# Parameter gradients of an S4 layer in a forward and backward kernel: two of their four groups computed during the second weights' gradient, from other buffers, with their scalings on VectorE

## The chip, the core and the metric

The kernel runs on one core of one Trainium2 chip. The metric is the device time of one execution in microseconds (us); of several executions the median counts, and less is better. A core has engines that work side by side, each in the order of its own instruction list: TensorE (PE in the profile, PEld for its weight loads), VectorE (DVE), ScalarE (ACT), GpSimd (POOL) and SyncE (SP). Here GpSimd and SyncE mostly issue DMAs, the transfers between the chip's memory (HBM) and the on-chip buffers (SBUF, 128 partitions). TensorE writes its results to banks of PSUM, from where VectorE or ScalarE must fetch them before a bank can be used again; such a fetch is called an evacuation.

## The reference, cut to what matters

A gated mixture of a state-space layer `a` and a two-layer network `b`, and the gradients of all its parameters:

```
g  = sigmoid((u * gate_w).sum(-1))                      # u: [1, 2048, 448] bf16
dt = exp(log_dt)[:, None];  A = A_re + i A_im; B, C likewise   # [448, 256]
K  = einsum("dn,dnl,dn->dl", C, exp(dt * A * l), dt * B).real
a  = irfft(rfft(u, 4096) * rfft(K, 4096))[:2048] + u * Dskip
b  = relu(u @ w1 + b1)**2 @ w2 + b2                     # 448 -> 1792 -> 448
y  = g * a + (1 - g) * b
outputs: y (out_0), and for a given grad_out the gradients of
u (out_1), A_re A_im B_re B_im C_re C_im (out_2..7), log_dt (out_8), Dskip (out_9),
w1 (out_10), b1 (out_11), w2 (out_12), b2 (out_13), gate_w (out_14)
```

What the change moves are out_2 to out_8. They are found for each of the 448 channels and 256 states from two complex sums over time, S and T, which the kernel has left in HBM earlier (s_d holds S and one part of T, t_d the other part), and from A, B, C and dt:

```
dB = dt*B;  W = C*dB                      (complex, 256 states wide)
dC = conj-product of dB and S;  dB-gradient = dt * conj-product of C and S
dA = dt * (W*T);   dlog_dt = sum over states of Re(W*S) + dt * Re(A*(W*T))
```

It is work for one elementwise engine: some 41 operations on tiles of 128 channels x 256 states, in four groups of 128, 128, 128 and 64 channels.

## The kernel before, in words

**How instructions get their order.** The kernel is written in a tile framework. A scheduler takes the program and lays down each engine's list: it follows the program's order as priority, but with its own estimate of times it may let a later instruction go first where an earlier one would wait. `tc.issue_after(x)` holds an instruction back in that schedule until x has been issued. Once laid down the order is fixed, and an engine stands still when the first instruction of its list has to wait. A buffer goes by a tag (`K.t("U16", ...)`): a new tile of the same tag may be written only when the last user of the old one is done.

**The stages.** Until some 660 us the kernel builds the convolution's kernel K and its spectrum, the network `b` and its hidden rows rT, the gradients' rows dhT, and the sums S and T. What the change touches comes after:

- The FFT of the kernel, fwd1 (L220) and fwd2 (L250), leaves the spectrum in the tile s1k. The end of fwd2 is interleaved with the products.
- `product(w, q)` (L1227): a complex multiplication of the spectra, `cmul` (L262 to L275, six VectorE operations of 128 x 1792 each), and `inv1` (L301), the first half of an inverse FFT on TensorE, whose result goes to HBM (hd, written from ScalarE's DMA queue). w is 0 for one of the two convolutions and 1 for the other, and q counts quarters. Products (0, 0..3) and (1, 0..1) stand in a row; products (1, 2) and (1, 3) stand in the loop of out_0.
- `grad_w2(j)` (L1180), j = 0 to 13, the second weights' gradient (out_12): `gradrows` (L1154) loads a block of rT by a 512 KB DMA from GpSimd's queue (L1166), TensorE turns it by 16 transposes (L1171), ScalarE squares it out of PSUM (L1172), TensorE does 16 matmuls (L1177) against the tile DB2, ScalarE copies the sum out (L1182), and GpSimd's queue stores it (L1183). VectorE has no part in it. DB2 lies in the buffer "U16".
- `grad_w1(j)` (L1186), j = 0 and 1: the same for the first weights, without the square. The other twelve blocks come at the very end.
- The parameter gradients' operands: A, B and C by twelve DMAs on GpSimd's queue (L1337, L1338: 192 KB for three groups together, 32 KB for the fourth) into the tile pgt, which takes over the buffer "U16" and so has to wait for the last matmul of grad_w2. `load_st` (L1235) brings s_d (512 KB a group) and t_d (256 KB) by SyncE's queue.
- `param_grads(dt)` (L1241): an add that completes T (L1250), two scalings of B by dt on ScalarE (L1261, L1262), the multiplications and additions on VectorE, two more scalings on ScalarE that write dA (L1271, L1272), the sum for dlog_dt, and six stores of 64 KB on GpSimd's queue (L1277). Groups 0 and 1 stand in the program after grad_w1(1) and ahead of the loop of out_0, groups 2 and 3 after that loop.
- The loop of out_0 (from L1356), four quarters: `inv2` (L325 to L332), the second half of the inverse FFT, of which the matmul L330 adds the network's part; and for each of four blocks of 128 rows two VectorE operations that read the bank (L1372, the row's dot product with grad_out, and L1373, the output). The text calls these "casts". A bank is free when both are done; two pairs of banks are in use.
- GU (L1389), one long multiplication on VectorE; then the loop of out_1, which is inv2 again with evacuations shared by ScalarE and VectorE (L1410); the turn of dlog (L1414), out_9 and out_14, and the other twelve blocks of grad_w1 (L1425 to L1433), half of each turned by a DMA transpose.

The scheduler weaves these together. In the trace the casts of out_0's first quarter run at 758.88, those of the second from 810.2, and the blocks of grad_w2 lie between them, one every 4.8 us. The scalings of group 0 stand in ScalarE's list among the evacuations of grad_w1, and the operations of group 0 in VectorE's list among the casts of out_0's third and fourth quarter.

Of the kernel before, what the change touches and what calls it, by code (L numbers as in the profile page):

```python
# [12 lines left out]
ACT = mybir.ActivationFunctionType  # L13
ALU = mybir.AluOpType
# [5 lines left out]
P = 128  # L20
L, D, N, F = 2048, 448, 256, 1792
LT = L // P
FT = F // P
DT = 4
# [313 lines left out]
def kernel(ctx, tc, A_u, A_A_re, A_A_im, A_B_re, A_B_im, A_C_re, A_C_im, A_log_dt, A_Dskip,  # L338
# [793 lines left out]
    K.pairs3 = False  # L1132
    K.fwd1(lambda j: xv[:, j], gd[2], stage= [b_[:, 1792 * i:1792 * i + 1792].rearrange("p (a d) -> p a d", d=D) for b_, n_ in ((Yv, 4), (Pk_, 4)) for i in range(n_)])
    lastw = row_block(3, ["X", "S", "F"])
    DB2 = K.t("U16", [P, LT, D])
    G_.dma_start(flat(DB2), bass.AP(tensor=DB_d, offset=0, ap=[[LT * D, P], [1, LT * D]]))
    U = K.t("D16", [P, LT, DP])
    G_.memset(U[:, :, D:D + 1], 1.0)
# [15 lines left out]
    def gradrows(w, j, nb):  # L1154

        nonlocal hi, ni
        late = w == 1 and j >= JL
        if late:
            raw_, hh = rl[hi % 2], hl[hi % 3]
            with tc.issue_after(lasths.ins):  # L1160
                nc.sync.dma_start_transpose(out=hh[:, 8:16], in_=bass.AP(tensor=dhT_d, offset=j * P * L + 1024, ap=[[L, P], [1, 1024]]))
        else:
            raw_, hh = hr[:, hi % 2], hn[:, hi % 2]
        hi += 1
        nl = L // 2 if late else L
        G_.dma_start(raw_, bass.AP(tensor=(rT_d if w == 0 else dhT_d), offset=j * P * L, ap=[[L, P], [1, nl]]))  # L1166
        for th in range(1 if late else 2):
            ps = K.ps(nb[ni % len(nb)], [P, 8, P], bf16)
            ni += 1
            for tt in range(8):  # L1170
                T_.transpose(ps[:, tt, :], raw_[:, (8 * th + tt) * P:(8 * th + tt + 1) * P], ident[:])  # L1171
            S.activation(hh[:, 8 * th:8 * th + 8, :], ps[:], ACT.Square if w == 0 else ACT.Copy)  # L1172
        ps = K.ps(nb[ni % len(nb)], [P, 512])
        ni += 1
        width = D if w == 0 else D + 1
        for t in range(LT):
            lastm = T_.matmul(ps[:, 0:width], lhsT=hh[:, t, :], rhs=(DB2[:, t, :] if w == 0 else U[:, t, 0:D + 1]), start=(t == 0), stop=(t == LT - 1))  # L1177
        return ps, lastm

    def grad_w2(j):  # L1180
        ps, lastm = gradrows(0, j, NB)
        S.copy(dw2s[:, j % 2], ps[:, 0:D])  # L1182
        G_.dma_start(out_12[j * P:(j + 1) * P, :], dw2s[:, j % 2])  # L1183
        return lastm
# [26 lines left out]
    def load_sx(w, q):  # L1211
        nonlocal nr
        t_ = ring[nr % 3]
        nr += 1
        nc.sync.dma_start(t_, bass.AP(tensor=sp_d[w], offset=q * 8 * D, ap=[[16 * 2 * D, P], [1, 8 * D]]))
        return t_.rearrange("p (a r d) -> p a r d", a=4, r=2)
# [10 lines left out]
    def product(w, q, sx):  # L1227
        K.cmul(Pk[:, q % 2], sx, spk(q), w == 1, Fc[:, 0:8 * D])
        K.inv1(Pk[:, q % 2], q, hd[1 + w])
# [11 lines left out]
    def param_grads(dt):  # L1241
        z = DSZ[dt]
        rows = slice(dt * P, dt * P + z)
        ob = Fc[:, 3584 + 1536 * (dt % 2):5120 + 1536 * (dt % 2)].rearrange("p (k n) -> p k n", k=6)
        ST, T1 = STs[dt], T1s[dt][:z]
        Ar, Ai, Br, Bi, Cr, Ci = (praw[:z, dt, i] for i in range(6))
        dBr, dBi, Wr, Wi, x1, x2, acc = (tmp[:z, i] for i in range(7))
        WTr, WTi = dBr, dBi
        V.tensor_tensor(out=ST[:z, 1], in0=ST[:z, 1], in1=T1, op=ALU.add)
        Sr, Si, Tr, Ti = ST[:z, 0, 0], ST[:z, 0, 1], ST[:z, 1, 0], ST[:z, 1, 1]  # L1250
        sc, nsc = dtc[:z, dt:dt + 1], ndtc[:z, dt:dt + 1]

        def mul(o_, a_, b_):
            V.tensor_tensor(out=o_, in0=a_, in1=b_, op=ALU.mult)  # L1254

        def sub(o_, a_, b_):
            V.tensor_tensor(out=o_, in0=a_, in1=b_, op=ALU.subtract)

        def stt(o_, a_, s_, b_, op1, **kw):
            V.scalar_tensor_tensor(out=o_, in0=a_, scalar=s_, in1=b_, op0=ALU.mult, op1=op1, **kw)  # L1260
        S.activation(dBr, Br, ACT.Copy, scale=sc)  # L1261
        S.activation(dBi, Bi, ACT.Copy, scale=sc)  # L1262
        mul(x1, Cr, dBr); mul(x2, Ci, dBi); sub(Wr, x1, x2)
        mul(x1, Cr, dBi); mul(x2, Ci, dBr); V.tensor_tensor(out=Wi, in0=x1, in1=x2, op=ALU.add)
        mul(x1, dBr, Sr); mul(x2, dBi, Si); sub(ob[:z, 4], x1, x2)
        mul(x1, dBr, Si); mul(x2, dBi, Sr); stt(ob[:z, 5], x1, -1.0, x2, ALU.subtract)
        stt(x1, Cr, sc, Sr, ALU.mult); stt(x2, Ci, sc, Si, ALU.mult); sub(ob[:z, 2], x1, x2)
        stt(x1, Cr, nsc, Si, ALU.mult); stt(x2, Ci, sc, Sr, ALU.mult); sub(ob[:z, 3], x1, x2)
        mul(x1, Wr, Tr); mul(x2, Wi, Ti); sub(WTr, x1, x2)
        mul(x1, Wr, Ti); mul(x2, Wi, Tr); V.tensor_tensor(out=WTi, in0=x1, in1=x2, op=ALU.add)  # L1270
        S.activation(ob[:z, 0], WTr, ACT.Copy, scale=sc)  # L1271
        S.activation(ob[:z, 1], WTi, ACT.Copy, scale=nsc)  # L1272
        mul(x1, Wr, Sr); mul(x2, Wi, Si); sub(acc, x1, x2)
        mul(x1, Ar, WTr); mul(x2, Ai, WTi); sub(x1, x1, x2)
        stt(x2, x1, sc, acc, ALU.add, accum_out=dlog[:z, dt:dt + 1])
        for i, o_ in enumerate((out_2, out_3, out_4, out_5, out_6, out_7)):
            G_.dma_start(o_[rows, :], ob[:z, i])  # L1277
# [2 lines left out]
    with tc.issue_after(last_s1.ins):  # L1280
        sx = [load_sx(0, q) for q in range(3)]

    Gt = K.t("Y16", [P, LT, D])
    for g in range(NG):
        nc.sync.dma_start(flat(Gt[32 * g:32 * g + 32]), tl(G2, g))
    brs = [RT[:, 10752 + 1792 * i:12544 + 1792 * i].rearrange("p (h x d) -> p h x d", h=2, x=2) for i in range(3)]
# [25 lines left out]
    def load_hs(w, q):  # L1312
        nonlocal nr
        hs = ring[nr % 3].rearrange("p (g x d) -> p g x d", g=4, x=2)
        nr += 1
        K.last_hs = K.load_hs(hd[w], q, hs)
        return hs
    sx = [load_sx(1, 0), load_sx(1, 1)]
    hsn = load_hs(1, 0)
    for q in range(2):  # L1320
# [2 lines left out]

    for j in range(FT):
        grad_w2(j)
        if j == 8:
            for g in range(NG):
                with tc.issue_after(last_s1.ins):
                    nc.sync.dma_start(U[32 * g:32 * g + 32, :, 0:D], tl(u2, g).rearrange("p (t d) -> p t d", d=D))
    for j in range(JS):  # L1330
        grad_w1(j, NB)

    pgt = K.t("U16", [P, 8192])

    praw = pgt[:, 0:6144].rearrange("p (k t n) -> p t k n", k=6, t=DT)
    for i, src in enumerate((A_A_re, A_A_im, A_B_re, A_B_im, A_C_re, A_C_im)):
        G_.dma_start(praw[:, 0:3, i], src[0:384, :].rearrange("(t p) n -> p t n", p=P))  # L1337
        G_.dma_start(praw[0:64, 3, i], src[384:448, :])  # L1338
    load_st(0, pgt[:, 6144:8192], SB[:, 11648:12672])
    load_st(1, M8[:, 0:2048], M8[:, 2048:3072])  # L1340
    param_grads(0)
    load_st(2, pgt[:, 6144:8192], SB[:, 11648:12672])
    param_grads(1)
    load_st(3, M8[:, 0:2048], M8[:, 2048:3072])
    negI = const.tile([P, P], bf16, name="negI")
    S.mul(negI[:], ident[:], -1.0)
    rcx, rcy = K.t("recx", [P, 1024]), K.t("recy", [P, 896])
# [8 lines left out]
    for q in range(4):  # L1356
        hs = hsn
        if q < 2:
            sx.append(load_sx(1, q + 2))
        if q == 2:  # L1360
            DX = K.t("P14", [P, 7168])
            dxq = [DX[:, 1792 * i:1792 * i + 1792].rearrange("p (a d) -> p a d", d=D) for i in range(4)]
        ao = oq[q] if q < 2 else dxq[q - 2]
        for x in range(2):
            pp = K.pair()
            for hp in range(2):
                t = 2 * q + x + 8 * hp
                ps = pp[hp][:, 0:D]
                br = brq[q][:, hp, x]
                K.inv2(hs, q, x, hp, ps, [(negI[:], br)])  # L1370
                jk = Fc[:, 6656 + 448 * (t % 2):7104 + 448 * (t % 2)]
                V.scalar_tensor_tensor(out=jk, in0=ps, scalar=1.0, in1=Gt[:, t, :], op0=ALU.mult, op1=ALU.mult, accum_out=dg[:, t:t + 1])  # L1372
                V.scalar_tensor_tensor(out=ao[:, 2 * hp + x], in0=ps, scalar=g32[:, t:t + 1], in1=br, op0=ALU.mult, op1=ALU.add)  # L1373
        if q < 3:
            hsn = load_hs(1, q + 1)
        brq.append(load_br((q + 3) // 4, (q + 3) % 4))
        if q < 2:
            product(1, q + 2, sx[q + 2])
        sl = lambda a: a[:].rearrange("p (h q x) -> p q h x", h=2, q=4)[:, q]
        V.tensor_copy(sl(dg_b), sl(dg))  # L1380
        V.tensor_tensor(out=sl(ds_b), in0=sl(dg_b), in1=sl(gp), op=ALU.mult)
        V.tensor_copy(sl(ds32), sl(ds_b))
        for g in range(NG):
            dst = bass.AP(tensor=o0.tensor, offset=o0.offset + (16 * g + 2 * q) * D, ap=[[64 * D, 32], [8 * D, 2], [1, 2 * D]])
            G_.dma_start(dst, ao[32 * g:32 * g + 32].rearrange("p (h x) d -> p h (x d)", h=2))
    param_grads(2)
    param_grads(3)
    GU = K.t("K28", [P, LT, D])
# [75 lines left out]
```

## Time and profile before

| | |
|---|---|
| device time, five runs | median 935.04 us (933.63 to 940.13) |
| profiled execution | 940.13 us, of which the span, from first to last instruction, is 938.3 |
| mean granted TensorE clock | 0.815 |
| TensorE (PE) busy | 727.8 us, 78% of the span, 7585 instructions |
| VectorE (DVE) busy | 671.0 us, 72%, 1148 |
| ScalarE (ACT) busy | 582.9 us, 62%, 931 |
| GpSimd (POOL) busy | 193.8 us, 21%, 335 |
| DMA | 184.97 MB, mean 197 GB/s |

The profile is a record of one execution: each instruction of each engine with its start and its length, each wait with what ended it, and each DMA. Four views of it are used. The page gives the sums above and the chain that ended last. A table of windows gives, for stretches of the span, how long each engine was busy in it and with how many instructions, the TensorE clock that the throttle granted as a share of full speed, and how busy the DMA engines were (a share can come out a little above 1). A timeline lists one engine's instructions: start in us, length in us, engine, line of the kernel, operation, the tiles written and read with their sizes, and in brackets how long the engine had been idle before it and what ended that. The chain of waits follows the last instruction back through what released it. Line numbers (L1177) are those of the listing above.

### The profile page before, as it was taken

Reading aid. Unit: us, or ns where it says so; the run is one execution under the profiler, and the core shown is the slowest. Engines: PE = TensorE matmul, PEld = TensorE weight load, DVE = VectorE, ACT = ScalarE, POOL = GpSimd, SP = SyncE. Lnnn points to the kernel's source line nnn. Section 1 sums busy time; section 2 is a strip of 40 time slices with the busy share of each in tenths; the row PEclk is TensorE's granted clock in tenths of the full one; section 3 lists DMA queues with packets and bytes.
Section 4 is the critical chain, followed back from the end, with each engine's and each line's share of the span. In section 5 each row is a group of like instructions: output and inputs, shape, how many; then the busy total and the mean of one; then the engine's idle time right before and its main releaser. Section 6 shows DMA issues by size and latency. Waiting matters only on the chain.

```text
span 938.3 us, 18852 instructions
## 1 busy us (share of the span) xinstructions
PE 727.8 (78%) x7585; PEld 343.9 (37%) x7585; DVE 671.0 (72%) x1148; ACT 582.9 (62%) x931; POOL 193.8 (21%) x335
## 2 busy tenths in 40 slices
PE   3637576556888898887888887889859888969895
PEld 1213222124344443434453442544323334523343
DVE  4659967796499999999887899664318954268810
ACT  3537847716978968789676755464526645436543
POOL 2330000102202121121202311223211021434220
PEclk9855655666959998999957997699979779968898
DMA  8996394895724776545844866449997997689862
GB/s 209 324 217 264 141 365 194 322 313 161 161 64 104 146 155 140 112 99 121 196 85 108 223 154 145 100 140 266 342 393 237 251 300 229 188 223 277 202 151 62
DMA packets 169631, 184.97 MB, mean 197 GB/s; under 512 B 100339, under 2 KB 146712, under 8 KB 168616
## 3 DMA queue, kind: packets, MB, share of 16 engines
q1 hardware_dynamic: 118710, 81.48, 36.2%
q0 software_dynamic: 21152, 67.46, 22.1%
q10 hardware_dynamic: 29682, 34.84, 11.7%
q8 instruction: 59, 0.97, 0.4%
q14 instruction: 28, 0.23, 0.1%
HBM read 88.22 MB, written 73.13 MB: 172 GB/s over the span
## 4 chain that ended last, share of the span: by engine, by line
PE 26%; ACT 20%; issue 20%; DMA 13%; DVE 13%; POOL 5%; SPq 2%; ACTq 0%; POOLq 0%; DVEq 0%
PE psN L1029 4%; PE psF L1177 3%; DMA S<-rT_d 2%; ACT R L925 2%; SPq L459 2%; PE psN L592 2%; PE psX L852 2%; ACT S L599 2%; POOL dhT_d L1105 2%; DMA prow<-in_B_b_dram 1%; DVE X L1254 1%; DMA hd<-st 1%; DMA DBT_d<-S 1%; DMA D<-hd 1%; ACT R L879 1%
## 5 line engine op out<-in xcount | busy, mean ns | idle before, releaser
L941 DVE TENSOR_TENSOR P<-R 128x2048 bf16<-128x2048 bf16 x42 | 49.6, 1219 | 25.9 <-ACT R L925 22.5
L925 ACT CAST R<-psF 128x1024 bf16<-128x1024 f32 x56 | 57.3, 1023 | 14.1 <-PE psF L921 14.1
L1177 PEld LDWEIGHTS <-S 128*128 128x128 bf16 x448 | 43.9, 104 | 59.5 <-issue 16.0
L1029 PE MATMUL psN<-D,S 128*128 128x448 bf16 x208 | 52.7, 386 | 4.7 <-ACT S L599 4.7
L1177 PE MATMUL psF<-U,S 128*128 128x448 bf16 x224 | 51.9, 382 | 2.1 <-ACT S L1172 2.0
L592 PE MATMUL psN<-S,U 128*128 128x512 bf16 x132 | 42.1, 438 | 8.3 <-ACT F L597 4.7
L921 PE MATMUL psF<-R,S 64*32 64x256 bf16 (+1 forms) x1344 | 38.8, 302 | 11.1 <-DMA R<-Y 6.5
L1092 PE MATMUL psN<-S,U 128*128 128x512 bf16 x126 | 38.8, 430 | 5.7 <-ACT D L1097 5.7
L208 DVE CAST K<-psN 128x448 bf16<-128x448 f32 x36 | 22.1, 623 | 29.4 <-PE psN L258 29.1
L781 DVE TENSOR_TENSOR X<-X,F 128x512 bf16<-128x512 bf16 (+1 forms) x70 | 37.5, 535 | 5.4 <-ACT F L815 3.5
L793 DVE TENSOR_TENSOR F<-K,F 128x2048 bf16<-128x2048 bf16 (+3 forms) x42 | 35.9, 855 | 4.6 <-ACT F L822 4.6
L1105 POOL DMA_DIRECT2D dhT_d<-D x28 | 20.2, 721 | 91.4 <-DVE D L1104 91.2
L792 DVE TENSOR_TENSOR K<-K,F 128x2048 bf16<-128x2048 bf16 (+3 forms) x42 | 36.4, 866 | 1.7
L258 PEld LDWEIGHTS <-M 128*64 128x64 bf16 x192 | 14.3, 131 | 63.5 <-issue 60.5
L782 DVE TENSOR_TENSOR F<-X,F 128x512 bf16<-128x512 bf16 (+1 forms) x70 | 37.0, 528 | 0.7 <-ACT F L816 0.2
L792 DVE TENSOR_TENSOR Y<-Y,F 128x2048 bf16<-128x2048 bf16 (+3 forms) x42 | 36.3, 865 | 1.5
L795 DVE TENSOR_TENSOR K<-K,F 128x2048 bf16<-128x2048 bf16 (+3 forms) x42 | 36.4, 866 | 1.3
L795 DVE TENSOR_TENSOR Y<-Y,F 128x2048 bf16<-128x2048 bf16 (+3 forms) x42 | 36.3, 865 | 1.3
L1029 PE MATMUL psN<-S,D 128*128 128x448 bf16 x168 | 36.2, 365 | 0.0
L891 ACT COPY M<-psX 128x1024 bf16<-128x1024 bf16 x26 | 26.4, 1017 | 15.4 <-PE psX L890 15.4
L793 DVE TENSOR_TENSOR F<-Y,F 128x2048 bf16<-128x2048 bf16 (+3 forms) x42 | 35.9, 855 | 0.1
L921 PEld LDWEIGHTS <-S 64*16 64x16 bf16 (+1 forms) x1792 | 22.4, 91 | 36.0 <-issue 30.5
(393 smaller groups left out, 1956.6 us busy)
## 6 DMA issues: line engine op xcount, KB each, us to landing
sp<-K ACTq DMA_DIRECT2D x8, 896.0 KB, 4.3
hd<-st ACTq DMA_DIRECT2D x16, 448.0 KB, 4.8
dhT_d<-D POOLq DMA_DIRECT2D x28, 256.0 KB, 5.5
R<-sp SPq DMA_DIRECT2D x8, 896.0 KB, 24.3
S<-rT_d POOLq DMA_DIRECT2D x14, 512.0 KB, 5.2
R<-hd SPq DMA_DIRECT2D x16, 448.0 KB, 6.5
rec_d<-F POOLq DMA_DIRECT2D x2, 1920.0 KB, 8.0
Y<-gd SPq DMA_DIRECT2D x4, 896.0 KB, 9.7
```

The costliest lines, as they stand in the source:

```text
L592: T_.matmul(ps[:], lhsT=w1w[:, dt, j * P:j * P + P], rhs=ub[:, dt], start=(dt == 0), stop=False, skip_group_check=True)
L781: V.tensor_tensor(out=hi4, in0=lo, in1=bcast_dims(pr, [0, (None, n), 1]), op=ALU.mult)
L792: V.tensor_tensor(out=hi, in0=lo, in1=bcast_dims(pr, [0, (None, n // 2), 1]), op=ALU.mult)
L793: V.tensor_tensor(out=Vv.rearrange("p (x a q) -> p x a q", x=rows, q=2), in0=lo, in1=bcast_dims(pi, [0, (None, n // 2), 1]), op=ALU.mult)
L795: return V.tensor_tensor(out=T4[:, :, :, n:2 * n], in0=T4[:, :, :, n:2 * n], in1=V4, op=ALU.add)
L921: T_.matmul(psz[32 * ii:32 * ii + m, t, 256 * s:256 * s + 256], lhsT=DKc[64 * t:64 * t + 64, s, g, 2 * ii:2 * ii + 1 + par].rearrange("p i ...
L925: S.copy(zb[:, :, :, gg].rearrange("p s t n -> p t s n"), psz[:].rearrange("p t (s n) -> p t s n", s=2))
L941: lastp = V.tensor_tensor(out=pr.rearrange("p s t g n -> p s t (g n)"), in0=zv, in1=(xb if r == 0 else rev_dim(xb, 2)), op=ALU.mult)
L1029: lastm = T_.matmul(ps[:, 0:D], lhsT=hblk[j][:, P * tt:P * tt + P], rhs=ws[:, j, :], start=(w == 1 and j == 0), stop=(j == FT - 1))
L1092: T_.matmul(ps[:], lhsT=w2Tw[:, jp, dt, j % 2], rhs=dblk[:, dt], start=(dt == 0), stop=False, skip_group_check=True)
L1105: G_.dma_start(bass.AP(tensor=dhT_d, offset=2 * p_ * P * L + 512 * lb, ap=[[L, P], [P * L, 2], [1, 512]]), hb)
L1177: lastm = T_.matmul(ps[:, 0:width], lhsT=hh[:, t, :], rhs=(DB2[:, t, :] if w == 0 else U[:, t, 0:D + 1]), start=(t == 0), stop=(t == LT - 1))
```

## The change

Both products (1, 2) and (1, 3) are now followed in the program by the parameter gradients of one group: `param_grads(0)` and `param_grads(1)` stand inside the first two passes of the loop of out_0, groups 2 and 3 after the loop as before.

Their operands no longer lie in "U16". A, B and C of groups 0 and 1 come, by twelve DMAs of 64 KB each on GpSimd's queue, into the unused ends of three buffers: columns 7168 to 8192 of XO for group 0 and 7552 to 8576 of Fc for group 1 (A and B), and the end of the tile that holds grad_out (C). They are issued after the rT load of grad_w2's fourth block. s_d and t_d of the two groups go by SyncE's queue to M8, SB and the end of DB2's buffer, from the same place in the program. The operands of groups 2 and 3 are loaded after the loop of out_0 into "U16" as before, by twelve DMAs of 64 and 32 KB.

The four scalings of every group are VectorE's now.

```diff
-    DB2 = K.t("U16", [P, LT, D])
+    DBv = K.t("U16", [P, 8192])
+    DB2 = DBv[:, 0:LT * D].rearrange("p (t d) -> p t d", d=D)
...
-        G_.dma_start(raw_, bass.AP(...))
+        K.last_raw = G_.dma_start(raw_, bass.AP(...))
...
-        Ar, Ai, Br, Bi, Cr, Ci = (praw[:z, dt, i] for i in range(6))
+        Ar, Ai, Br, Bi, Cr, Ci = (x[:z] for x in praw[dt])
...
-        S.activation(dBr, Br, ACT.Copy, scale=sc)
-        S.activation(dBi, Bi, ACT.Copy, scale=sc)
+        V.tensor_scalar(out=dBr, in0=Br, scalar1=sc, scalar2=None, op0=ALU.mult)
+        V.tensor_scalar(out=dBi, in0=Bi, scalar1=sc, scalar2=None, op0=ALU.mult)
...
-        S.activation(ob[:z, 0], WTr, ACT.Copy, scale=sc)
-        S.activation(ob[:z, 1], WTi, ACT.Copy, scale=nsc)
+        V.tensor_scalar(out=ob[:z, 0], in0=WTr, scalar1=sc, scalar2=None, op0=ALU.mult)
+        V.tensor_scalar(out=ob[:z, 1], in0=WTi, scalar1=nsc, scalar2=None, op0=ALU.mult)
...
-    Gt = K.t("Y16", [P, LT, D])
+    Gv = K.t("Y16", [P, 8192])
+    Gt = Gv[:, 0:LT * D].rearrange("p (t d) -> p t d", d=D)
...
+    A_all = (A_A_re, A_A_im, A_B_re, A_B_im, A_C_re, A_C_im)
+    praw = {dt: [b_[:, o_ + 256 * i:o_ + 256 * i + 256] for i in range(4)]
+            + [Gv[:, 7168 + 512 * dt + 256 * i:7424 + 512 * dt + 256 * i] for i in range(2)]
+            for dt, b_, o_ in ((0, XO, 7168), (1, Fc, 7552))}
...
     for j in range(FT):
         grad_w2(j)
+        if j == 3:
+            for dt in range(2):
+                for i, src in enumerate(A_all):
+                    with tc.issue_after(K.last_raw.ins):
+                        G_.dma_start(praw[dt][i], src[dt * P:dt * P + P, :])
+            load_st(0, M8[:, 0:2048], SB[:, 11648:12672])
+            load_st(1, M8[:, 2048:4096], DBv[:, 7168:8192])
...
-    pgt = K.t("U16", [P, 8192])
-    praw = pgt[:, 0:6144].rearrange("p (k t n) -> p t k n", k=6, t=DT)
-    for i, src in enumerate((A_A_re, A_A_im, A_B_re, A_B_im, A_C_re, A_C_im)):
-        G_.dma_start(praw[:, 0:3, i], src[0:384, :].rearrange("(t p) n -> p t n", p=P))
-        G_.dma_start(praw[0:64, 3, i], src[384:448, :])
-    load_st(0, pgt[:, 6144:8192], SB[:, 11648:12672])
-    load_st(1, M8[:, 0:2048], M8[:, 2048:3072])
-    param_grads(0)
-    load_st(2, pgt[:, 6144:8192], SB[:, 11648:12672])
-    param_grads(1)
-    load_st(3, M8[:, 0:2048], M8[:, 2048:3072])
...
         if q < 2:
             product(1, q + 2, sx[q + 2])
+            param_grads(q)
...
+    pgt = K.t("U16", [P, 8192])
+    pg = pgt[:, 0:3072].rearrange("p (k t n) -> p t k n", k=6, t=2)
+    for dt in (2, 3):
+        praw[dt] = [pg[:, dt - 2, i] for i in range(6)]
+        for i, src in enumerate(A_all):
+            G_.dma_start(praw[dt][i][0:DSZ[dt]], src[dt * P:dt * P + DSZ[dt], :])
+    load_st(2, pgt[:, 3072:5120], pgt[:, 5120:6144])
+    load_st(3, M8[:, 0:2048], SB[:, 11648:12672])
     param_grads(2)
     param_grads(3)
```

In the lists that the scheduler makes of the changed program, 28 operations of group 0 stand in VectorE's list ahead of the first cast of out_0, its first two among the third product of w = 0 and the add within the fourth; the rest of group 0, products (1, 2) and (1, 3), GU and group 1 stand between the casts of the first and the second quarter. The order of TensorE's list is nearly the same as before; 8 transposes and 8 matmuls of grad_w2's fifth block have come to stand ahead of the first quarter's inv2, and the transposes of grad_w1(2) ahead of the third quarter's. The first two scalings and two multiplications of group 2 stand on VectorE ahead of the last cast of the second quarter. On SyncE's queue the s_d loads of groups 0 and 1 and their t_d loads stand ahead of the three u loads that remain and of the first hd load of out_0. On GpSimd's queue the first twelve operand loads stand ahead of grad_w2's fifth rT load, and the other twelve where the old ones did, followed by the third dhT load.

More of the change, by code (lines that the diff above doesn't have):

```diff
@@ L1165, in gradrows @@
         nl = L // 2 if late else L
-        G_.dma_start(raw_, bass.AP(tensor=(rT_d if w == 0 else dhT_d), offset=j * P * L, ap=[[L, P], [1, nl]]))
+        K.last_raw = G_.dma_start(raw_, bass.AP(tensor=(rT_d if w == 0 else dhT_d), offset=j * P * L, ap=[[L, P], [1, nl]]))
         for th in range(1 if late else 2):
@@ L1317, in load_hs @@
         return hs
+    A_all = (A_A_re, A_A_im, A_B_re, A_B_im, A_C_re, A_C_im)
+    praw = {dt: [b_[:, o_ + 256 * i:o_ + 256 * i + 256] for i in range(4)] + [Gv[:, 7168 + 512 * dt + 256 * i:7424 + 512 * dt + 256 * i] for i in range(2)]
+            for dt, b_, o_ in ((0, XO, 7168), (1, Fc, 7552))}
     sx = [load_sx(1, 0), load_sx(1, 1)]
```

## The prediction

> **What bounds the kernel now.** The page came first: TensorE 727.8 us busy of 938.3, VectorE 671.0, and a chain shared by everything (PE 26%, ACT 20%, issue 20%). Such an average can't price a move between two stages, so I cut the last 218 us at the places where VectorE changes its work, and asked for the windows.
>
> ```profile
> core 0: us, PE busy (x) PEld busy (x) DVE busy (x) ACT busy (x) POOL busy (x), PEclk, DMA share, GB/s
> 720.00:750.30 30.30, 26.20 (x133) 8.68 (x132) 29.43 (x31) 21.88 (x44) 1.66 (x4) 0.83 0.94 256
> 750.30:758.90 8.60, 6.61 (x38) 2.37 (x36) 0.03 (x2) 3.95 (x9) 1.09 (x2) 0.79 1.07 364
> 787.60:810.20 22.60, 21.98 (x172) 12.50 (x169) 0.00 (x0) 13.54 (x21) 4.66 (x9) 1.00 0.58 178
> 810.20:828.40 18.20, 14.13 (x97) 7.22 (x97) 5.93 (x16) 8.43 (x15) 10.75 (x19) 0.87 0.87 227
> 828.40:854.40 26.00, 20.25 (x119) 7.98 (x118) 23.71 (x68) 9.29 (x20) 8.86 (x16) 0.70 0.83 249
> 854.40:896.00 41.60, 35.95 (x230) 15.10 (x227) 35.95 (x95) 25.47 (x60) 14.17 (x26) 0.92 0.88 216
> 896.00:938.00 42.00, 31.00 (x208) 16.68 (x208) 0.02 (x1) 17.50 (x43) 7.71 (x13) 0.94 0.39 97
> ```
>
> VectorE is the bound in 720 to 750 (29.43 of 30.30: the products), idle for 22.60 us in 787 to 810 while TensorE runs grad_w2 without a gap at full clock, and the bound again in 828 to 854, where TensorE has gaps and its clock falls to 0.70. From 896 TensorE works alone. So a microsecond of VectorE work is free in the third row, costs in the first, and earns in the fifth. The timelines of ScalarE, TensorE and VectorE show how 810 to 854 is lost:
>
> ```profile
> 823.70 0.51 ACT L1261 ACTIVATE X<-U,dtc 128x256 f32<-128x256 bf16 x1 [4.12 <-DMA U<-in_A_B_re_dram]
> ```
> ```profile
> 825.78 5.47 PE L1177 MATMUL psX<-D,S 128*128 128x449 bf16 x16 [4.07 <-ACT S L1200]
> ```
> ```profile
> 828.43 0.42 DVE L1254 TENSOR_TENSOR X<-U,X 128x256 f32<-128x256 bf16 x1 [6.92 <-DMA U<-in_A_C_re_dram]
> ```
> ```profile
> 839.24 0.55 PE L330 MATMUL psN<-R,negI 128*128 128x448 bf16 x1 [2.90 <-DVE P L1373]
> ```
>
> ScalarE stands 4.12 us in front of one scaling whose operand has not landed; the evacuations that TensorE needs are queued behind it. Then TensorE runs 16 matmuls in 5.47 us that take 3.21 at 815.79. VectorE then works through group 0, with the casts of out_0's third and fourth quarter strewn between its 41 operations and 14 of group 1, and TensorE waits for the banks.
>
> **The change, part by part.** Sums are against the profiled execution (span 938.3, time 940.1).
>
> *Cost of a group.* Group 3 has VectorE from 882.65 to 895.8: 13.2 us; group 2 about 14. ScalarE's four scalings take 0.51 us each. On VectorE the nearest row is L566, a tensor_scalar of 128x448, median 0.33; I take 0.4 each, 1.6 a group (0.3 to 0.5: twice the columns, but float32 here).
>
> One of the L566 rows took 2.35 us (at 63.78), under four GpSimd memsets. The Trainium skill, "SBUF — State Buffer", "Who interferes with whom", says that a tensor_scalar in a two-port mode and a GpSimd operation lock each other out, which speaks against putting scalings on VectorE. By that row eight scalings moved would cost 8 x 2.0 = 16 us; but GpSimd issues only DMAs there, 0.54 us each, so the rule gives at most 8 x 0.54 = 4 us, 1 us of it where VectorE is the bound. I take 0 and keep 1 for the range.
>
> *Group 0 in the products.* In the changed order 28 instructions of group 0 stand before out_0's first cast: 2 scalings among the third product and the rest from the fourth on. 26 at 0.42, one add of 0.69, the scalings: 12.3 us. The gap of 8.57 us before 758.88 takes most of it: the casts start at 750.3 + 12.3 = 762.6 and end near 767.5, 4 us late. TensorE needs them then, since its inverse stage trails the products, which end 5.6 us late. But its order now has 8 matmuls and 8 transposes of grad_w2 ahead of those casts (2.1 to 4 us). Net, TensorE is 1.5 us late at 779. It stays so: until 817 it runs back to back, and the late products feed inverse matmuls that stand 5 us apart between grad_w2 blocks. Cost +1.5 (0 to +6).
>
> *Rest of group 0, and group 1.* After 767.5: 13 operations (5.9), two products (13.3), the product GU (3.9), group 1 (14 + 1.6): 38.7 us, ending near 806, before the next cast at 811.7. Hidden with 5 us to spare; beyond it every microsecond would be paid. The wait of 6.29 us for R<-sp at 777 goes (that load is out before 770), but was off the path: 0.
>
> *Loads.* On POOL twelve 64 KB loads now go out at 711, ahead of the fifth rT load (719.51) and a dW2 store: 12 x 0.54 = 6.5 us and some waiting for landings; that rT load leaves by 725 and is used after 745. The other twelve go out where the old ones did, at 814. The Trainium skill, "DMA: Bandwidth & Descriptors", "Bandwidth", says to batch, transfers under 64 KB being dominated by descriptors; by the fit of its "Anatomy of one DMA — SWDGE (gpsimd) path", 2.0 us plus bytes over 436e3, 24 loads of 64 KB cost 2.15 each where 6 of 192 cost 2.45. In the trace the 64 KB stores took 4.5 to landing, the 192 KB loads 4.0 to 8.2. As fixed cost in series the rule makes the change some 22 us dearer; overlapped, and 100 us ahead of need or in no worse place than before, I put it at 0. On SP the s_d and t_d loads of groups 0 and 1 now stand ahead of the u loads (727.89) and the first hd load (744.84), and wait for fwd2's last matmul (729.9). u is needed only at GU; the hd load still waits longer for its own data. The add of group 0 falls at 737.6; its s_d has 7 us to land, the hd stores there take 2.8 to 8.5. I take no stall (0 to +6, kept in the range). SP no longer issues s_d among out_1's loads (1.1 us at 863.89). Twelve gradient stores of 64 KB move to 757 to 815, with POOL mostly idle: 0.
>
> *ScalarE's stall goes.* 4.07 us of idle TensorE and 2.26 of slow clock, 6.3. What is late next: group 2's two scalings and two multiplies now stand on VectorE before the last cast of the second quarter, waiting for the same DMAs (near 825). That cast moves from 820.5 to 826.2; TensorE needs its bank only after the 16 matmuls, at 828. I take -5.
>
> *Third and fourth quarter.* From 826.2: 23 operations of group 2 (9.1), then 16 casts without a stranger between (2 x 4.6): 844.9, against 854.4 before. Two things take back part: the third dhT load stands behind all twelve new loads, about 1 us; and TensorE ends its part after the casts. It starts out_1 near 846.5, against 853.4: -7, the lag of +1.5 and the -5 included.
>
> *out_1 and the tail.* out_1 took 27 us, paced by the hd ring (one wait of 2.87). It moves as a whole, with 1 us less from SP: -8. From there TensorE is the bound as before; the dlog transpose, for which it waited 0.37, comes with VectorE done at 862 instead of 896.
>
> Sum: 938.3 - 8 = 930.3, or 932 of the profiled execution. That one is the slowest of the five, 5.1 over the median of 935.04[...]. I take -7 on the median: **928**, own range 922 to 931.
>
> **Rivals.**
> *Eaten early: 934.* The lag of the products is 5 to 6 us rather than 1.5, and VectorE's new wait for group 2 replaces ScalarE's. For: the DMA share is already 0.94 to 1.07 there, and 1.3 MB more comes into 711 to 745. Against: 8.57 idle on VectorE right behind the products. -7 + 4 to 6: about 934.
> *Slower: 941.* One mechanism: the add of group 0 waits for s_d inside the fourth product. VectorE is in order, so that product's last step, two more products, the casts and TensorE's inverse stage all stand behind it. For: s_d follows a 896 KB load on SP, and such loads took up to 24.3 us. Against: that was at 673, with five of them queued. Each microsecond of waiting is one lost, plus up to 2 of slow clock; 7 us undo the gain, and from 12 the kernel is slower: 14 give 935 - 7 + 13 = 941.
> *Group 1 does not fit before 810.* Needs over 5 us of VectorE waits between 768 and 806; it shares its price with the first rival.
>
> **How the numbers follow.** Forecast 0.58, eaten 0.20, slower 0.22. A measurement of this kernel can tell about 0.5% from no change (4.7 us), so "same" is 930.4 to 939.7. Of the forecast 0.54 lies under 930.4, and 0.01 of the early rival; of the slower case 0.06 stays under 939.7. So faster 0.55, same 0.27, slower 0.18. The range takes the early rival and the slower case's lower half: 921 to 940, leaving 0.06 below and 0.13 above.
>
> **What would show it.** Right: group 0 among the products, no wait over 2 us at its add; VectorE done with group 1 before out_0's second quarter; no ScalarE wait for in_A_B; no 16 matmuls of 5.4 us near 825; out_1 starting 7 us earlier after the lag at 779 of 1 to 2. Wrong: VectorE waiting for s_d near 737; TensorE waiting for VectorE in 780 to 815; out_1 starting where it did.

## The result, and the profile after

The changed kernel takes 927.66 us, the median of 29 runs (921.93 to 940.87), against 937.07 for the kernel before in 50 runs: a ratio of 0.9916, 95% interval 0.9896 to 0.9936. A ratio leaves out the runs that lie more than 1.5% above the fastest of their kernel, which the medians keep; e5's profiled execution, in the second table below, is such a run. The profiled execution of the changed kernel has a span of 928.4 us.

The table of windows for the changed kernel, cut again where VectorE changes its work:

```profile
core 0: us, PE busy (x) PEld busy (x) DVE busy (x) ACT busy (x) POOL busy (x), PEclk, DMA share, GB/s
720.00:753.40 33.40, 28.80 (x141) 9.67 (x139) 32.97 (x50) 20.88 (x40) 4.29 (x8) 0.79 0.89 253
753.40:765.20 11.80, 4.33 (x22) 1.77 (x21) 0.00 (x0) 1.60 (x4) 0.00 (x0) 0.64 1.04 338
765.20:803.60 38.40, 36.26 (x272) 19.67 (x270) 37.76 (x76) 22.10 (x34) 13.88 (x26) 0.94 0.78 235
803.60:820.90 17.30, 17.30 (x134) 9.27 (x132) 3.61 (x11) 10.01 (x16) 8.31 (x16) 1.00 0.74 213
820.90:844.10 23.20, 17.94 (x106) 7.18 (x105) 20.07 (x57) 6.97 (x16) 10.51 (x19) 0.78 0.87 243
844.10:863.40 19.30, 17.01 (x129) 7.37 (x128) 18.42 (x55) 14.56 (x34) 7.53 (x14) 1.00 0.98 261
863.40:928.00 64.60, 51.33 (x327) 24.99 (x325) 0.00 (x0) 26.20 (x62) 8.81 (x15) 0.91 0.54 126
```

VectorE is now busy for 37.76 us of the 38.40 in which grad_w2 runs beside it, where it had 22.60 us with nothing, and it is done at 863.4, not at 896. So the move does what it says. The second row got worse: VectorE stood still there before too (0.03 us busy of the 8.60 in row 750.30 of the table before), but TensorE worked for 6.61 of them and ScalarE for 3.95. Now VectorE has no work for 11.80 us, of which ScalarE works for 1.60 and TensorE for 4.33, while the DMA engines are full.

The timelines of ScalarE, TensorE and VectorE in that row, one line each:

```profile
763.60 0.53 ACT L207 CAST st<-psN 128x448 bf16<-128x448 f32 x1 [10.57 <-DMA hd<-st]
```
```profile
764.18 0.53 PE L330 MATMUL psN<-R,negI 128*128 128x448 bf16 x1 [7.47 <-ACT st L207]
```
```profile
765.26 0.62 DVE L1372 SCALAR_TENSOR_TENSOR F<-psN,Y 128x448 bf16<-128x448 f32 x1 [11.90 <-PE psN L332]
```

Read from the top: ScalarE can't empty a bank of product (1, 1), because its staging buffer `st` is still being written to hd (the DMA issued at 748.00 took 15.5 us to land). TensorE, in order, waits for that bank ahead of out_0's first quarter, and VectorE waits for TensorE. The text calls this wait of ScalarE's the staging wait. Before, the longest was 4.69:

```profile
754.22 0.53 ACT L207 CAST st<-psN 128x448 bf16<-128x448 f32 x1 [4.69 <-DMA hd<-st]
```

The stall that the prediction began with is gone. TensorE's second block of grad_w1, which was `825.78 5.47` after 4.07 us of idle time, now starts without a wait and takes 3.21:

```profile
820.27 3.21 PE L1178 MATMUL psX<-D,S 128*128 128x449 bf16 x16
```

and the wait for in_A_B_re stands on VectorE instead:

```profile
821.09 0.35 DVE L1262 TENSOR_SCALAR X<-U,dtc 128x256 f32<-128x256 bf16 x1 [5.72 <-DMA U<-in_A_B_re_dram]
```

The two profiled executions can't simply be subtracted: they come to the first matmul of grad_w2 at 704.5 (before) and 699.4 (after), a difference of 5.1 us that arose in code that the change doesn't touch. This table therefore counts from that matmul, for all kernels below but e10. The later columns are less the start in the second: out_0 and out_1 by their first L330, the blocks of grad_w1 by their first matmul, VectorE by the end of its last operation for dlog, the end by the span. Each row is one execution.

| kernel | grad_w2 starts | out_0 starts | grad_w1(0) | grad_w1(1) | out_1 starts | VectorE done | end |
|---|---|---|---|---|---|---|---|
| before | 704.5 | 53.3 | 111.3 | 121.3 | 149.0 | 191.6 | 233.8 |
| changed | 699.4 | 64.8 | 115.2 | 120.9 | 144.3 | 164.0 | 229.0 |
| e1 scalings only | 699.8 | 54.7 | 114.4 | 120.0 | 153.3 | 197.1 | 238.2 |
| e2 move only | 696.7 | 55.2 | 107.6 | 120.1 | 137.5 | 166.8 | 228.1 |
| e3 one group | 693.1 | 65.0 | 121.4 | 127.0 | 146.7 | 183.3 | 236.0 |
| e4 all late | 692.9 | 53.6 | 112.1 | 117.8 | 140.6 | 199.8 | 240.5 |
| e5 as e4, dlog last | 706.6 | 52.6 | 108.0 | 113.7 | 139.0 | 199.7 | 230.0 |
| e6 no weave | 695.9 | 62.5 | 116.5 | 122.6 | 139.9 | 162.2 | 227.0 |
| e7 third stage | 696.9 | 51.2 | 103.8 | 109.9 | 128.9 | 149.8 | 213.3 |
| e8 groups 2, 3 held | 702.8 | 58.7 | 109.3 | 114.9 | 136.3 | 166.2 | 218.8 |
| e9 before, third stage | 697.8 | 52.6 | 108.8 | 119.9 | 142.5 | 190.7 | 231.9 |
| e11 stage and hold | 701.3 | 51.3 | 104.9 | 110.9 | 125.5 | 157.2 | 211.5 |
| e12 as e11, no weave | 695.0 | 50.5 | 106.0 | 111.6 | 130.4 | 161.8 | 214.3 |

### The profile page after: what moved, and what is told of

The parts are those of the page before. It is cut to its first block, busy times and chain, and to the rows that moved or that the text cites. A ratio compares the mean times of both kernels' runs of the same rounds, so it can differ in the third digit from the quotient of the medians.

```text
span 928.4 us, 18868 instructions
## 1 busy us (share of the span) xinstructions
PE 723.4 (78%) x7585; PEld 342.1 (37%) x7585; DVE 671.4 (72%) x1164; ACT 577.2 (62%) x915; POOL 198.6 (21%) x347
## 4 chain that ended last, share of the span: by engine, by line
PE 30%; ACT 20%; issue 17%; DMA 14%; DVE 11%; POOL 4%; SPq 2%; ACTq 0%; POOLq 0%; DVEq 0%
PE psF L1178 5%; PE psN L1029 3%; DMA hd<-st 3%; ACT R L925 2%; SPq L459 2%; PE psN L592 2%; ACT S L599 2%; PE psN L1178 2%; POOL dhT_d L1105 2%; DMA S<-rT_d 2%; DMA prow<-in_B_b_dram 1%; PE psX L852 1%; DMA DBT_d<-S 1%; DMA D<-hd 1%; DMA dk_d<-st 1%
## 5 line engine op out<-in xcount | busy, mean ns | idle before, releaser
L258 PEld LDWEIGHTS <-M 128*64 128x64 bf16 x192 | 14.6, 135 | 64.8 <-issue 61.6
```

## The experiments

All ratios are to the kernel before, run beside it on the same chip. e6, e7, e8 and e10 to e12 had six runs each, the others 14 to 22. e1 to e4 ask where the gain comes from; the theory then was the prediction's (ScalarE's stall, and "strangers" among the casts: operations of the groups that stand between them in VectorE's list).

**e1, the scalings alone.**

```diff
 before.py
-        S.activation(dBr, Br, ACT.Copy, scale=sc)      # and the other three
+        V.tensor_scalar(out=dBr, in0=Br, scalar1=sc, scalar2=None, op0=ALU.mult)
```

> The kernel before with the four scalings of each group on VectorE and nothing else. Theory (the gain is ScalarE's wait for in_A_B, some 5 us, and the strangers between out_0's last casts, some 5 us): the first half of the gain, 931 to 935, with no ScalarE wait of 4 us before L1261 and no 16 matmuls of 5.4 us near 825; the groups still stand among the casts of the third and fourth quarter. Rival (the gain is VectorE work taken out of the last third): nothing is taken out and VectorE has some 6 us more there, so 937 or more.

938.81 us, ratio 0.9998 (0.9966 to 1.0029): nothing, as the rival had it. The stall is gone (grad_w1(1) follows grad_w1(0) after 5.7 us, 10.0 before), and TensorE loses the time at the next place. Its timeline at the fourth quarter of out_0:

```profile
837.57 0.55 PE L330 MATMUL psN<-R,negI 128*128 128x448 bf16 x1 [8.82 <-DVE P L1373]
```

Before, that wait was 2.90. VectorE stands in front of the same loads (5.17 us for in_A_B_re at 822.23) and then works through group 0, and the casts come as late as ever.

**e2, the move alone.**

```diff
 after.py
-        V.tensor_scalar(out=dBr, in0=Br, scalar1=sc, scalar2=None, op0=ALU.mult)      # and the other three
+        S.activation(dBr, Br, ACT.Copy, scale=sc)
```

> The changed kernel with the scalings back on ScalarE. Theory: groups 0 and 1 are done early, but group 2's scalings stand in ScalarE's list again and wait there for in_A_B near 820, with the evacuations of grad_w1 behind them: 4 to 5 us come back, 931 to 933. Rival (work taken out of the last third): as fast as the changed kernel, 927 to 929.

930.97 us, ratio 0.9926 (0.9897 to 0.9955): not told apart from the whole gain, though by the medians it is 5.9 us where the changed kernel has 9.4. The stall that the theory expected is there, in ScalarE's timeline:

```profile
813.35 0.51 ACT L1262 ACTIVATE X<-U,dtc 128x256 f32<-128x256 bf16 x1 [6.93 <-DMA U<-in_A_B_re_dram]
```

and grad_w1(1) follows after 12.5 us. But the order differs too: with its scalings on ScalarE group 0 isn't woven into the products, the staging wait is 4.32, and out_0 starts at 55.2, not 64.8. So the scalings' place decides where time is lost, and in sum nothing that these runs can tell.

**e3, one group early instead of two.**

```diff
 after.py, the early loads for group 0 alone
-            param_grads(q)
+            if q == 0:
+                param_grads(0)
...
+    param_grads(1)      # loaded into "U16" with groups 2 and 3
     param_grads(2)
     param_grads(3)
```

> The changed kernel with group 0 alone early; group 1 is loaded into U16 and computed with groups 2 and 3. In the order of the lists its operations come to stand behind the last cast of out_0. Theory: what counts is what stands ahead of the casts, and that is as in the changed kernel: 927 to 930. Rival (work taken out of the last third): half of the gain, 932 to 933.

934.17 us, ratio 0.9975 (0.9949 to 1.0001): about a third of the gain, and its interval reaches no change. That is against the theory and nearer to the rival. The early staging wait is the same (ScalarE 10.81), VectorE is done at 183.3, not at 164.0, and TensorE now waits 1.75 us for dlog.

**e4, nothing early, all groups behind the casts.**

```diff
 before.py, scalings on VectorE
-    param_grads(0)
-    param_grads(1)      # with the loads between them
...
+    with tc.issue_after(lc.ins):      # lc: the last cast of out_0
+        param_grads(0)      # the loads between them as before
+        param_grads(1)
         param_grads(2)
         param_grads(3)
```

> The kernel before with the scalings on VectorE and all four groups held behind the last cast of out_0, so nothing is early: VectorE works through them while TensorE has out_1 and the last blocks of grad_w1. Theory: no stall and no strangers, so about the whole gain without the move, 927 to 932; up to 3 us may be lost where SyncE's loads of s_d wait for a group to end. Rival (work taken out of the last third): no gain, 937 or more.

940.17 us, ratio 1.0021 (0.9991 to 1.0052): no gain. out_1 starts at 140.6, earlier than in the changed kernel, and all of it is given back in the tail, which takes 99.8 us from there to the end, where it takes 84.8 before. VectorE is done 8.2 us later than before, and TensorE meets it at the turn of dlog:

```profile
885.03 3.21 PE L1177 MATMUL psN<-D,S 128*128 128x449 bf16 x16 [1.11 <-ACT S L1172]
892.80 0.22 PE L1415 MATMUL psN<-ident,dlog_b 128*4 128x128 bf16 x1 [4.56 <-DVE dlog_b L1413]
```

The turn of dlog needs all four groups; behind it, in TensorE's list, stand the rest of grad_w1 and the last stores, 40.6 us. It costs more than the 4.56 us: in the 9.2 us behind the wait the granted clock was 0.63, and the next 16 matmuls took 4.54 us. The wait isn't all of the longer tail either, since e4 starts out_1 with half a block more of grad_w1 still to do. In the kernel before the same line tells that this date was just met:

```profile
896.08 0.22 PE L1414 MATMUL psN<-ident,dlog_b 128*4 128x128 bf16 x1 [0.37 <-DVE dlog_b L1412]
```

From this the theory changed: VectorE has two dates. The casts must be early, so that out_1 starts, and the last group must be done 41 us before the end. Without the move, in both orders that were run (before and e4), one date is late or only just met. e5 tests this; e6 to e8 test the new wait and group 2's place.

**e5, e4 with dlog's turn last.**

```diff
 e4
-    dlog_b = const.tile([P, 4], bf16, name="dlog_b")      # copy, transposition, two stores
...
     for j in range(JL, FT):
         grad_w1(j, NB + NT[0:4])
+    dlog_b = const.tile([P, 4], bf16, name="dlog_b")      # the same, in another bank
```

> The kernel of e4 with the turn of dlog (the small transposition that needs every group, and its two stores of out_8) put last, behind all of grad_w1. In e4 TensorE came to it at 888 and stood 4.56 us, until VectorE had ended the fourth group at 892.8. Theory, new: VectorE has two dates, the casts that let out_1 start and dlog, whose turn stands some 41 us before the end in TensorE's list; before the change one of the two is always late. Then with the second date gone e4's early out_1 counts: 929 to 934. Rival (VectorE's work in the last third costs by itself, by its stores on GpSimd's queue ahead of the dhT loads): 937 or more, as e4.

930.22 us, ratio 0.9919 (0.9890 to 0.9948): by the ratio the whole gain of the change, by the medians 5.6 of its 9.4 us, with no group early and no other buffers. From e4 it differs by one small transposition put elsewhere; TensorE now comes to it last, and it isn't VectorE that it waits for:

```profile
927.81 0.22 PE L1426 MATMUL psS<-ident,dlog_b 128*4 128x128 bf16 x1 [0.57 <-ACT S L1200]
```

In the table VectorE is done as late as in e4 (199.7 and 199.8), and the end comes 10.5 us earlier. The intervals of e4 and e5 lie apart, so in e4's order the second date was worth about 1%. What dlog's place alone would give the kernel before, or the changed one, was not run.

**e6, group 0 behind the products.**

```diff
 after.py
-            param_grads(q)
+            with tc.issue_after(lcm.ins):      # lcm: the last multiplication of product (1, 1)
+                param_grads(q)
```

> The changed kernel with group 0 held behind the last multiplication of product (1, 1), so that nothing of it stands among the products. Theory: the weaving costs about 6 us at the first quarter of out_0 (there TensorE was idle 7.47 us and ScalarE 10.57), of which about half is taken back before 784; held, 2 to 4 us faster than the changed kernel, 923 to 926. Rival (TensorE waits there for the DMAs of hd, whatever VectorE does): 927 to 929.

923.09 us, ratio 0.9885 (0.9847 to 0.9923), which overlaps with the changed kernel's interval. The time came out as the theory had it, its place did not: ScalarE's staging wait is 12.24 us, TensorE's at the first quarter 11.75, longer than with the weave:

```profile
758.40 0.53 PE L330 MATMUL psN<-R,negI 128*128 128x448 bf16 x1 [11.75 <-ACT st L207]
```

out_0 starts at 62.5. So it isn't the weave that makes that wait; in the profiled execution the gain comes after grad_w1(1), where out_1 follows after 17.3 us against 23.4.

**e7, a third staging buffer.**

```diff
 after.py
     hsn = load_hs(1, 0)
+    K.st_more = [oq[1]]      # 1792 columns of XO, used by out_0's second quarter later
     for q in range(2):
         product(1, q, sx[q])
+    K.st_more = []
```

> The changed kernel with a third staging buffer for the hd writes of products (1, 0) and (1, 1), in columns of XO that out_0 needs only later. ScalarE stood 10.57 us there because a staging buffer had not been written out. Theory: that wait goes, TensorE's idle time at the first quarter of out_0 shrinks from 7.47 to below 4, and 1 to 3 us of it remain at the end: 924 to 927. Rival (TensorE's own operand, the hd load, is as late as the staging): no change, 927 to 929.

912.88 us, ratio 0.9786 (0.9740 to 0.9831): by the medians 15 us below the changed kernel, by the ratios 12, where 1 to 3 were expected. ScalarE has no wait for a staging buffer left, and out_0 starts without one:

```profile
748.11 0.44 PE L330 MATMUL psN<-R,negI 128*128 128x448 bf16 x1
```

By the table the 13.6 us gained at out_0's start are 11.0 at grad_w1(1) and 15.4 at out_1. The 1 to 3 came from the thought that the rT loads would hold TensorE up in any case, as before the change (2.86 us at 778.64); the longest such wait in e7, from out_0's start to its second quarter, is 0.80.

**e8, groups 2 and 3 behind the casts.**

```diff
 after.py
-    param_grads(2)
-    param_grads(3)
+    with tc.issue_after(lc.ins):
+        param_grads(2)
+        param_grads(3)
```

> The changed kernel with groups 2 and 3 held behind the last cast of out_0. In the changed kernel group 2's first operations wait 5.72 and 1.32 us for in_A ahead of a cast of the second quarter, and 23 of them stand ahead of the third quarter's; TensorE idles 2.50 and 2.74 us for it. Theory: both go, VectorE ends near 870 where dlog is asked for at 888, so 3 to 5 us faster than the changed kernel: 923 to 925. Rival (TensorE would wait there for the next dhT load instead, since GpSimd issues it at 823): no change, 927 to 929.

923.59 us, ratio 0.9878 (0.9836 to 0.9919), in the theory's range, though the interval still overlaps with the changed kernel's. Theory and rival both said something true: TensorE does meet the dhT load there,

```profile
826.30 1.04 PE L1172 MATMUL psF<-ident,S 128*128 128x128 bf16 x8 [3.16 <-DMA S<-dhT_d]
```

but it has no wait for a bank of the casts after it, where the changed kernel has this one:

```profile
835.51 0.56 PE L330 MATMUL psN<-R,negI 128*128 128x448 bf16 x1 [2.74 <-DVE P L1373]
```

The dlog date is met with 0.88 us of waiting. The table's 10.2 us at the end are not all the hold's: this execution was already 6.1 us ahead at out_0's start, where VectorE's order is still that of the changed kernel, because ScalarE's staging wait was 6.37 and not 10.57. So that wait differs by some 4 us between executions of one order. From grad_w1(1) to out_1 it gains 2.0.

**e9, the third staging buffer in the kernel before.** The edit of e7.

> The kernel before with the third staging buffer of e7 and nothing else. e7 came out 15 us below the changed kernel. Theory (the change itself brought most of that wait: ScalarE stood 4.69 us for a staging buffer before and 10.57 after): 2 to 4 us faster than before, 932 to 935. Rival (the staging was as much a brake before, and the change has nothing to do with it): 920 to 925.

931.50 us, ratio 0.9947 (0.9920 to 0.9974), half a per cent: just beyond the theory's range, far from the rival. With it the change would be worth 0.9916 x 0.9947 = 0.9863 if the two were independent; together they give 0.9786. The surplus, 0.0077 of 937 or 7 us, fits what the timelines have (ScalarE's wait is 10.57 us in the changed kernel and 4.69 before), but the product is uncertain by some 0.003 and e7's ratio by 0.0045, so that the surplus is hardly clear of nothing. That the wait grew with the change is seen in the traces (though not in e2's, 4.32); its price is known only roughly.

**e10, other turns of the ring.**

```diff
 after.py
     hsn = load_hs(1, 0)
+    nr += 2
```

> The changed kernel with the ring's buffers taken in another turn, so that the 896 KB load of sp for product (1, 2) must wait for the first quarter of out_0, and the next hd load behind it on SyncE's queue too. In the changed kernel they are issued at 748 to 752, just when the hd writes that ScalarE waits for are on their way; before they went out at 754 and later. Theory (those loads slow the hd writes): ScalarE's 10.57 us and TensorE's 7.47 shrink to below 5, and the kernel is 2 to 8 us faster than the changed one, 920 to 926, if product (1, 2) isn't late for it. Rival (the writes are slow for another reason): the wait stays, 927 or more.

928.39 us, ratio 0.9876 (0.9815 to 0.9937). The edit isn't what its text says: the sp load comes to stand in the program ahead of the first quarter that still needs the buffer, so that the first quarter of out_0 is computed from sp's data, and its matmuls L332 run at 785.20, 15 us behind the first L330. ScalarE's wait is 8.16 us. It tells nothing on what makes the hd write slow.

**e11 and e12, both together, and with e6.** The edits of e7 and e8, and in e12 that of e6 too.

> The changed kernel with e7's third staging buffer and e8's hold of groups 2 and 3. Theory (two waits in different places): the gains add, 15 and 4: 906 to 910. Rival (with the first quarter early, TensorE meets GpSimd's and SyncE's loads instead): 911 to 915.

> e11 with group 0 also held behind the products, as in e6. Theory (the weave delays the products, and so the first quarter): 2 to 4 us below e11, 903 to 908. Rival (e6's gain came from what stands ahead of the casts of the later quarters, which e11 has already): as e11, 906 to 910.

916.65 us, ratio 0.9793 (0.9735 to 0.9852), and 915.83, 0.9789 (0.9736 to 0.9842). Neither is told apart from e7, so the gains of 15 and 4 don't add, and e11's 906 to 910 was missed. In e7 TensorE's waits for casts are down to 0.77, 0.88 and 0.78 us already, so there is little for the hold to take away, and e11's TensorE meets an hd load at out_1 (2.71 us). e7 with its one edit is as good as anything that was run, 12 to 15 us below the changed kernel.

## Why the prediction was right, point by point

The time came out: 928 was forecast and 927.66 measured. The 7 us taken off the median stand against 9.4 by the medians and 7.9 by the ratio. To meet the number within 0.4 us was luck: the median of the kernel before itself went from 935.04 in five runs to 937.07 in fifty, and several terms missed by 1 to 2 us. The place came out too: VectorE's work left the last third for the 22.60 us in which it had stood idle. Of the steps, not all held.

- *The scalings.* 0.34 to 0.47 us each in the trace, 0.4 taken. The Trainium skill's rule that VectorE and GpSimd can lock each other out ("SBUF — State Buffer", "Who interferes with whom"), by which the prediction's estimate was at most 4 us, showed no such price: the scalings that overlapped one of GpSimd's DMA issues took 0.35 us (at 772.89) to 0.47 (at 800.24). The 0 held.
- *Group 0 in the products.* The last of its 28 operations ended at 753.36, 54.0 after the start of grad_w2, against the 58.1 that the prediction's 762.6 means. VectorE was earlier than thought, and the casts, at 65.9, later (58.1). The step that failed is "Net, TensorE is 1.5 us late": at grad_w1(0) it is 3.9 late. The prediction saw the full DMA engines and asked only whether s_d, the u loads and the hd loads would be late; the hd writes go out in the same stretch, and ScalarE waits for those by way of two staging buffers. No wait for s_d stood at L1250; the rival that was slower by it didn't come.
- *Loads.* 0 was taken against an estimate of 22 us. The first twelve landed in 3.3 to 6.7 us (median 4.9), the last of them issued at 713.42, and nothing waited for them. By the fit of the Trainium skill ("DMA: Bandwidth & Descriptors", "Anatomy of one DMA — SWDGE (gpsimd) path") the prediction had estimated 2.15 us for each; the measured time is longer, and ahead of need it cost nothing. The other twelve took 3.3 to 7.9, where the old ones took 4.0 to 8.2, and VectorE waited 5.72, 0.93 and 1.32 us for three of them, as the prediction had it for group 2.
- *Group 1 hidden.* It ended at 803.6, ahead of the next cast at 809.03: right. The wait for R<-sp went too; that it was worth nothing was not shown.
- *ScalarE's stall.* -5 was taken; from grad_w1(0) to grad_w1(1) it is -4.3. As a size right, as a cause of the gain not: e1 has that saving too and is no faster than before, e2 lacks it and isn't told apart from the changed kernel. It is one of several waits in a row, of which the next takes over.
- *Third and fourth quarter.* From grad_w1(1) to out_1 27.7 us became 23.4. TensorE still waits 2.50 us and then 2.74 for casts, ahead of which group 2 stands. All told out_1 starts 4.7 us earlier, where 7 was forecast.
- *The tail.* 84.8 became 84.7, not 1 less.
- *The sum.* By these terms -4.8 in the last stage, where the median says -9.4. e1, whose time is that of the kernel before, needs 238.2 us for the stage; the profile of before had 233.8. One profiled execution of each doesn't size the stage to better than these 4.4 us: against e1's 238.2 the change is worth -9.2 there. The -8 of the sum lies between the two.
- *"The dlog transpose, for which it waited 0.37"* was named and set aside. e4 and e5 show that it was a second date: a wait of 0.37 us was a tie, not slack, and in e4, where VectorE is done 8.2 us later, it was worth about 1%.
- *Slips in the sums.* 28 operations with two scalings and one add come to 12.0 us, not 12.3; 826.2 + 9.1 + 9.2 is 844.5, not 844.9; of the 24 loads six are of 32 KB, and twelve loads more at 2.0 us are 24 us, not 22; the slower rival's 14 us of waiting enter its sum as 13; and the parts named for "same" and "slower" add up to 0.29 and 0.16, not 0.27 and 0.18. None of them moves the forecast by more than 0.4 us.

The first rival, eaten early, came half true (a new wait of 7.47 us) with another mechanism, and was covered by what VectorE no longer did late. Which part of the gain the first date has and which the second, the runs don't say for the changed kernel: e1 shows that the scalings alone give nothing, e2 that the move carries the gain, e5 that about as much can be had without it.

What stays open: why the hd write at 748.00 took 15.5 us to land, where the hd transfers of that stretch took at most 8.5 before the change. In the changed kernel SyncE issues the sp load at 748.28 and the next hd loads from 750.25, before at 754.61 and 765.15; that these slow the write was argued and not shown. The kept traces go with it: ScalarE's longest staging wait was 6.37 to 12.24 us in the four kernels in which SyncE had begun to issue those hd loads when the wait began (changed, e3, e6, e8), and 4.32 to 6.04 in the five in which they came only as it ended or later (before, e1, e2, e4, e5). That is no proof, since the executions differ in more, and among the four the wait varies by 6 us. Nor was it shown what moves out_1 in e6; there the waits for casts are 0.88 and 0.78 us where the changed kernel has 2.50 and 2.74.

## What to carry to other kernels

An engine's work has a date for each result that someone waits for, and a tiny wait on such a result (0.37 us here) can mean that it only just isn't late; before moving work early, try holding it late and putting behind other work the one consumer that sets the date, as e5 does. A stall that is taken away is worth what the next wait in line leaves, so take it away alone and measure. When loads are moved into a stretch in which the DMA engines are full, ask which stores leave a staging buffer there, and who waits for that buffer.

## What the runs showed that was not expected

Of 16 equal 448 KB writes to hd in the changed kernel, which landed in 4.7 us in the median, one took 15.5, and one buffer more for them was worth some 12 to 15 us there, more than the whole change, and 5 to 6 in the kernel before. After some waits TensorE ran slow for some microseconds: 16 matmuls took 3.20 to 3.21 us in a row, but 4.95 after the waits of e2's stall (2.59 and 2.68 us, granted clock 0.64) and 4.76 after one of 2.97 us in e4 (0.66). And a stretch ahead of all that was edited can shift a profiled execution by more than the change does: the kernels here came to grad_w2 between 692.9 and 708.4.
